# Own buffers for the opening's loads, output decay on the outputs and a reordered slot in a retention plus softplus-FFN kernel

## The chip, the core and the metric

The kernel runs on one core of a Trainium2 chip. The metric is the device time of one execution in microseconds (us). Three timed runs of the kernel before gave 914.02 to 916.24 us, median 914.99 us. A hardware profile of one further execution is read below; that execution took 915.2 us.

The engines, with the names the profile uses: PE (TensorE matmul; PEld is its weight load), DVE (VectorE), ACT (ScalarE), POOL (GpSimd) and SP (SyncE, which here issues every DMA). Each engine executes its own instruction list strictly in order, so an instruction that waits holds everything behind it on that engine.

## The reference

```python
scores = (q @ k.T) / sqrt(64)                    # 8 batches, 8 heads, 576 positions, head size 64
ret    = scores * gamma[h] ** (i - j)  (0 where j > i)
attn   = ret @ v
x      = attn.transpose(0, 2, 1, 3).reshape(4608, 512)
h      = x @ w_in                                # 512 -> 2048
g      = max(h, 0) + log1p(exp(-abs(h)))         # softplus
out    = g @ w_out                               # 2048 -> 512
```

All in float32. The decay gamma^(i-j) factors into gamma^(i+1), which belongs to the query position, and gamma^-(j+1), which belongs to the key/value position.

## The kernel before

**Attention** is done in *steps*: 36 chunks of 128 tokens times two halves of the heads give 72 steps. A step m loads one block `raw` of 128x1152 floats (keys, queries, keys by position, values; 576 KB). On PE it needs `scores` (lines 150 and 155: eight 64x64 score products and up to eight state sums k'v, all into one PSUM tile) and `values` (lines 204 and 214: scores times v, then queries times the carried state). DVE turns the score tile into the masked `a` (L168) and the sums into `u`, `sx` and the carried state `s` (L181 to L193); POOL copies half of the old state into `sx` (L177) and decays `s` (L195). `values_out` writes the result as a rounded head (ACT, L229) and the remainder (DVE, L233) into `xt`, the input of the FFN. `scale_next` multiplies the queries (L127) and, from step 9 on, the values (L130) by their decay factors on POOL, in place in `raw`; for steps 0 to 8 ACT scales the values (L140).

**The FFN** runs in 144 *slots*, 16 for each unit of 512 tokens. Slot i does 12 matmuls `h` (L248), then Abs, Exp, Ln on ACT (L256 to L258), the softplus sum on DVE (L262), a rounded head `g` on ACT (L266) and its remainder on DVE (L267). After the `h` matmuls of slot i, PE does the 12 `y` matmuls (L280) of slot i-1. In every odd slot one attention step is put ahead of `h`: scores of step m, values of step m-1.

**The weights** come as 32 pieces of 512 KB in a raw form. Each piece passes `weight_a` (ACT Prelu L309, DVE L311), `weight_b` (DVE L317), `weight_c` (ACT head L325) and `weight_d` (DVE remainder L330). In the text below these are p (L309), t (L311), b, c and d. Three raw buffers `wst` take turns; the load of piece n+3 is issued behind d of piece n. Pieces 0 to 2 begin in the opening; slot i handles pieces 3+2i and 4+2i, so slots 0 to 14 carry weight work.

**The stages.** The *opening* is steps 0 to 8 before slot 0. The *weight slots* are slots 0 to 14. The *plain slots* follow. The order of the work is written out by hand: the program order of each engine is the order of the source. Opening blocks take turns in three `rawp` buffers and two `g` buffers, so a load waits until the block that lay there is used.

Of the kernel before, what the change touches and what calls it, by code (L numbers as in the profile page):

```python
# [19 lines left out]
P = 128  # L20
# [15 lines left out]
SMALL = 2 * QC  # L36
NCONST = NPAIR * QC + H + NPAIR
PIECE = 512
START_WEIGHTS = 3
OPENING = 5  # L40
WBUFS = 3
# [17 lines left out]
def retention_softplus_ffn(ctx: ExitStack, tc, first, others, consts, w, out):  # L59
    nc = tc.nc  # L60

    const = ctx.enter_context(tc.tile_pool(name="const", bufs=1))
    wpool = ctx.enter_context(tc.tile_pool(name="wpool", bufs=1))
    xpool = ctx.enter_context(tc.tile_pool(name="xpool", bufs=2))
    att = ctx.enter_context(tc.tile_pool(name="att", bufs=2))
    moe = ctx.enter_context(tc.tile_pool(name="moe", bufs=2))
# [3 lines left out]
    ps_h = ctx.enter_context(tc.tile_pool(name="ps_h", bufs=2, space=PSUM))  # L70
    ps_att = ctx.enter_context(tc.tile_pool(name="ps_att", bufs=1, space=PSUM))
    rawp = ctx.enter_context(tc.tile_pool(name="rawp", bufs=3))
    weight_pools = ExitStack()
    wst = weight_pools.enter_context(tc.tile_pool(name="wst", bufs=WBUFS))
    later = {}

    consts_sb = const.tile([P, NCONST], F32, name="consts_sb")
    mask = const.tile([P, HC], F32, name="mask")

    decq = [consts_sb[:, n:n + SMALL].rearrange("p (s c) -> p s c", s=2) for n in (0, NCONST - SMALL)]  # L80
    vsc, gchp = consts_sb[:, SMALL:SMALL + H], consts_sb[:, SMALL + H:SMALL + H + NPAIR]


    ws = [wpool.tile([P, 2, 2 * PIECE], F32R, name=f"w{p}") for p in range(NF)]
# [17 lines left out]
    def load_step(m):  # L102

        pool, tag = (moe, "g") if m in (3, 4, 8) else (rawp, "rawp")
        r = pool.tile([P, RAW], F32, tag=tag, name=f"raw_{tag}")
        if m == 0:
            for to, at in ((consts_sb, slice(0, SMALL + H + NPAIR)), (r, slice(0, KQ)), (r, slice(KQ, RAW)),
                           (consts_sb, slice(NCONST - SMALL, NCONST))):
                nc.sync.dma_start(to[:, at], (first if to is r else consts)[:, at])
        else:  # L110
            nc.sync.dma_start(r, others[m - 1])
        kq, kv = r[:, 0:KQ], r[:, KQ:]
        k = kq[:, 0:2 * C].rearrange("p (s c) -> p s c", s=2)
        q = kq[:, 2 * C:].rearrange("p (s c) -> p s c", s=2)
        kv = kv.rearrange("p (a s c) -> p a s c", a=2, s=2)
        live[m] = dict(k=k, q=q, kp=kv[:, 0], v=kv[:, 1])

    scaled = [0]

    def scale_next():  # L120

        m = scaled[0]
        if m not in live:
            return
        scaled[0] += 1
        q = live[m]["q"]
        nc.gpsimd.tensor_mul(q, q, decq[m % 2])  # L127
        if m >= AHEAD:
            v, f = value_scale(m)
            nc.gpsimd.tensor_mul(v, v, f.unsqueeze(2).broadcast_to([P, 4, D]))  # L130

    def value_scale(m):
        return live[m]["v"].rearrange("p s (h d) -> p (s h) d", h=2), vsc[:, 4 * (m % 2):4 * (m % 2) + 4]

    def scale_values(m):

        if m < AHEAD:
            v, f = value_scale(m)
            for n in range(4):
                nc.scalar.activation(v[:, n], v[:, n], AF.Copy, scale=f[:, n:n + 1])  # L140

    def scores(m, bank):

# [4 lines left out]
        for s in range(2):  # L148
            for t, h in quads:
                nc.tensor.matmul(bank[rows[t], h, SCOLS][:, part[s]], L["k"][rows[h], s, part[t]],  # L150
                                 L["q"][rows[h], s, part[t]], start=True, stop=True, skip_group_check=True)
        for s in range(2):
            for t, h in quads:
# [353 lines left out]
```

## Time and profile before

| what | value |
|---|---|
| median of three timed runs | 914.99 us |
| the profiled execution: own time / span of the trace | 915.2 us / 913.5 us |
| busy share: PE / PEld / DVE / ACT / POOL | 98% / 80% / 41% / 48% / 18% |
| h matmuls: count, busy | 1740, 426.1 us |
| y matmuls: count, busy | 1728, 415.9 us |
| HBM read / written | 59.64 MB / 9.44 MB |

The shares are averages over stages with different limits: PE is short of work only in the first 130 us. The stage table and the chain of waits in the rows below show that.

### The profile page before, as it was taken

To read this page: it belongs to the slowest core of one execution; us is meant where nothing else is said; L and a number is where in the kernel's file an instruction comes from. 1 tells how busy PE (TensorE), PEld (TensorE's weight loads), DVE (VectorE), ACT (ScalarE), POOL (GpSimd) and SP (SyncE) were. 2 spreads that over 40 slices of the span, in tenths; PEclk is the share of its full clock that TensorE was granted. 3 is DMA by queue.
4 is the path that set the end of the run, shared out by engine and by line. 5 is a ranking of instruction groups with operands and counts; after the bars stand their busy time and mean duration, and the time that the engine had idled before them with its cause. 6 is when DMAs were issued, how large, how long until landed. Compare 5 with 4: busy or idle time off the path is not lost.

```text
span 913.5 us, 18133 instructions
## 1 busy us (share of the span) xinstructions
PE 892.7 (98%) x7830; PEld 726.4 (80%) x7830; DVE 376.1 (41%) x745; ACT 440.9 (48%) x775; POOL 164.8 (18%) x270
## 2 busy tenths in 40 slices
PE   7699999999999999999999999999999999999998
PEld 6577778888888888888888888888888888888886
DVE  5689984333333343333433343334333333332222
ACT  5577774444444444444444444444444444445444
POOL 5322221111111111111221111111211121100000
PEclk7799999999999999999999999999999999999999
DMA  8556642111211112111211121112111121001001
GB/s 289 204 187 213 206 153 98 36 45 52 99 52 53 53 66 65 48 53 52 99 53 52 52 80 48 52 54 99 52 53 53 39 88 53 27 1 47 1 1 46
DMA packets 20671, 70.24 MB, mean 77 GB/s; under 512 B 2288, under 2 KB 2544, under 8 KB 20592
## 3 DMA queue, kind: packets, MB, share of 16 engines
q1 hardware_dynamic: 20592, 69.09, 22.9%
q8 instruction: 61, 1.00, 0.5%
q14 instruction: 18, 0.15, 0.1%
HBM read 59.64 MB, written 9.44 MB: 76 GB/s over the span
## 4 chain that ended last, share of the span: by engine, by line
PE 88%; DVE 5%; DMA 3%; ACT 3%; POOL 1%; issue 0%; SPq 0%; POOLq 0%; DVEq 0%; ACTq 0%
PE h L248 41%; PE y L280 40%; PE bank L150 2%; DMA raw_rawp<-others 2%; PE bank L214 2%; PE bank L204 2%; PE bank L155 1%; DMA wst<-w 1%; DVE g L267 1%; DVE wst L317 1%; DVE w L330 1%; DVE wst L311 1%; ACT w L325 1%; POOL raw_rawp L127 1%; DVE ab L262 0%; ACT ab L257 0%
## 5 line engine op out<-in xcount | busy, mean ns | idle before, releaser
L248 PE MATMUL h<-xt,w 128*128 128x512 f32 (+1 forms) x1740 | 426.1, 394 | 0.9 <-DVE w L330 0.8
L280 PE MATMUL y<-w,g 128*128 128x512 f32 x1728 | 415.9, 390 | 3.1 <-DVE g L267 3.1
L280 PEld LDWEIGHTS y<-w,g 128*128 128x128 f32 x1728 | 323.7, 188 | 73.2 <-DVE g L267 5.3
L248 PEld LDWEIGHTS h<-xt,w 128*128 128x128 f32 x1740 | 320.3, 188 | 71.7 <-DVE w L330 3.3
L262 DVE SCALAR_TENSOR_TENSOR ab<-h,ab 128x512 f32<-128x512 f32 (+1 forms) x145 | 99.7, 688 | 408.2 <-ACT ab L258 408.1
L256 ACT ACTIVATE ab<-h 128x512 f32<-128x512 f32 (+1 forms) x145 | 86.3, 595 | 295.1 <-PE h L248 295.1
L267 DVE TENSOR_TENSOR g<-ab,g 128x512 fp32r<-128x512 f32 (+1 forms) x145 | 104.2, 718 | 90.7 <-ACT g L266 89.2
L266 ACT CAST g<-ab 128x512 fp32r<-128x512 f32 (+1 forms) x145 | 89.5, 617 | 100.1 <-DVE ab L262 98.8
L127 POOL TENSOR_TENSOR raw_rawp<-raw_rawp,consts_sb 128x384 f32<-128x384 f32 x69 | 72.3, 1048 | 193.1 <-DMA raw_rawp<-others 186.7
L195 POOL TENSOR_TENSOR s<-s,consts_sb 128x128 f32<-128x128 f32 x64 | 25.7, 401 | 419.7 <-DVE s L193 372.4
L258 ACT ACTIVATE ab<-ab 128x512 f32<-128x512 f32 (+1 forms) x145 | 91.2, 629 | 4.6
L257 ACT ACTIVATE ab<-ab 128x512 f32<-128x512 f32 (+1 forms) x145 | 91.2, 629 | 4.6
L130 POOL TENSOR_TENSOR raw_rawp<-raw_rawp,consts_sb 128x256 f32<-128x256 f32 x63 | 41.5, 659 | 0.0
L229 ACT CAST xt<-bank 128x256 fp32r<-128x256 f32 x68 | 25.3, 372 | 30.4 <-PE bank L214 30.3
L150 PEld LDWEIGHTS bank<-raw_rawp 64*64 64x64 f32 x1008 | 20.4, 133 | 22.2 <-issue 22.2
L214 PE MATMUL bank<-raw_rawp,sx 64*64 64x64 f32 x472 | 27.8, 221 | 4.3 <-POOL sx L177 4.3
L204 PE MATMUL bank<-a,raw_rawp 64*64 64x64 f32 x1056 | 30.6, 223 | 0.0
L168 DVE TENSOR_TENSOR a<-bank,mask 128x256 f32<-128x256 f32 x63 | 26.6, 423 | 9.6 <-ACT xt L229 9.5
L233 DVE TENSOR_TENSOR xt<-bank,xt 128x256 fp32r<-128x256 f32 x68 | 28.3, 416 | 3.8 <-ACT xt L229 3.7
L150 PE MATMUL bank<-raw_rawp 64*64 64x64 f32 x1008 | 29.1, 230 | 0.0
L309 ACT ACTIVATE wst<-wst 128x512 f32<-128x512 f32 x32 | 21.8, 682 | 13.3 <-DMA wst<-w 13.3
L155 PE MATMUL bank<-raw_rawp 64*64 64x64 f32 x888 | 25.9, 218 | 0.0
(74 smaller groups left out, 422.4 us busy)
## 6 DMA issues: line engine op xcount, KB each, us to landing
raw_rawp<-others SPq DMA_DIRECT2D x68, 576.0 KB, 4.1
wst<-w SPq DMA_DIRECT2D x32, 512.0 KB, 3.9
out<-osb SPq DMA_DIRECT2D x36, 256.0 KB, 2.4
raw_g<-others SPq DMA_DIRECT2D x3, 576.0 KB, 7.8
raw_rawp<-first SPq DMA_DIRECT2D x1, 320.0 KB, 3.1
raw_rawp<-first SPq DMA_DIRECT2D x1, 256.0 KB, 4.4
consts_sb<-consts SPq DMA_DIRECT2D x1, 198.0 KB, 2.3
consts_sb<-consts SPq DMA_DIRECT2D x1, 192.0 KB, 4.6
```

The lines of the kernel that those rows point to most:

```text
L127: nc.gpsimd.tensor_mul(q, q, decq[m % 2])
L150: nc.tensor.matmul(bank[rows[t], h, SCOLS][:, part[s]], L["k"][rows[h], s, part[t]], L["q"][rows[h], s, part[t]], start=True, stop=True, s ...
L204: nc.tensor.matmul(o[t][rows[h], part[s]], L["v"][rows[t], s, rows[h]], L["a"][rows[t], h, s], start=(s == 0), stop=L["states"][t] is None ...
L214: nc.tensor.matmul(o[t][rows[h], part[s]], lhs[rows[t], s], rhs, start=False, stop=True, skip_group_check=True)
L248: nc.tensor.matmul(h, ws[p][:, a, kt * P:(kt + 1) * P], xt[:, b, kt, cols], start=(n == 0), stop=(n == 3 * NKT - 1))
L256: nc.scalar.activation(ab, h, AF.Abs)
L257: nc.scalar.activation(ab, ab, AF.Exp, scale=-1.0)
L258: nc.scalar.activation(ab, ab, AF.Ln, bias=1.0)
L262: nc.vector.scalar_tensor_tensor(ab, h, 0.0, ab, op0=ALU.max, op1=ALU.add)
L266: nc.scalar.copy(g[:, HI], ab)
L267: nc.vector.tensor_sub(g[:, LO], ab, g[:, HI].bitcast(F32))
L280: nc.tensor.matmul(y, g[:, a, at:at + P], ws[p][:, b, PIECE:], start=(p == 0 and n == 0), stop=(p == NF - 1 and n == 2))
```

## The change

1. **Loads of the opening.** Steps 0 to 10 get buffers of their own (`openp`, `NOPEN` = 11), at the place in SBUF where weight tiles 8 to 15 are put later, once step 11 is reached. Step 0 and the constants it needs come as two DMAs, `part0` and `part1`. From step 11 on two `rawp` buffers (before: three) take turns, and the load of step m+1 is issued in the slot of step m.
2. **Decay on the outputs.** The POOL multiplication of the queries (L127 before, 128x384, 72 of them) is gone. `values_out` now multiplies the PSUM result by the decay on DVE into a tile `x` (128x256); ACT rounds the head from `x`, and the remainder is subtracted on POOL (on DVE for step 7 alone).
3. **Four raw weight buffers** (before: three); pieces 0 to 3 are loaded in the opening.
4. **Order of a slot.** In the weight slots t of piece n+1 is moved up next to b of piece n, the step's DVE work stands behind the softplus sum instead of ahead of the slot, and d of piece n-1 stands between the logarithm and the softplus sum. In the plain slots the step's DVE work stands behind `h` in the program.
5. PE does the same instructions in the same order, with three idle matmuls at the start instead of five.

```diff
-OPENING = 5
-WBUFS = 3
+OPENING = 3
+NOPEN = AHEAD + 2
+WBUFS = 4
 def load_step(m):
-        pool, tag = (moe, "g") if m in (3, 4, 8) else (rawp, "rawp")
-        r = pool.tile([P, RAW], F32, tag=tag, name=f"raw_{tag}")
...
+            if m < NOPEN:
+                r = openp.tile([P, RAW], F32, name=f"raw{m}")
+            else:
+                r = rawp.tile([P, RAW], F32, tag="rawp", name="rawp")
...
-    def scale_next():
...
-        q = live[m]["q"]
-        nc.gpsimd.tensor_mul(q, q, decq[m % 2])
...
+    def values_out(m, bank, rest):
...
+        x = att.tile([P, 2, C], F32, tag="x", name="x")
+        nc.vector.tensor_mul(x.rearrange("p s (t c) -> p s t c", t=2),
+                             bank[:, :, VCOLS].rearrange("p t (s c) -> p s t c", s=2),
+                             constant[0][2][:, pr:pr + 2].rearrange("p s (t c) -> p s t c", t=2))
+
+        def parts_out():
+            nc.scalar.copy(hi, x)
+            rest.tensor_sub(lo, x, hi.bitcast(F32))
+        return parts_out
...
     for i in range(NSLOT):
+        weight_p(n)
+        weight_t(n)
+        weight_c(n - 1)
+        weight_b(n)
+        weight_t(n + 1)
         h = hidden_mm(i)
         ab = logs(h)
+        weight_dl(n - 1)
         softplus(h, ab)
-        weight_cd(n)
+        if step and n < NPIECE:
+            parts_out = values_out(m - 1, bank, nc.gpsimd)
+            scores_out(m)
+            states_out(m)
+            if NOPEN <= m + 1 < NSTEP:
+                load_step(m + 1)
+            scale_values(m + 1)
+        weight_c(n)
+        weight_dl(n)
         gs[i] = [softplus_split(ab)]
-        weight_a(n + 1)
+        softplus_rest(gs[i][0], ab)
+        if step and n < NPIECE:
+            parts_out()
+        weight_p(n + 1)
         weight_b(n + 1)
```

The order of the instructions at two places. First POOL at the end of the opening, before. The names ending in a number are buffers: `raw_rawp_478` is the block of step 9, `sx_545` the state half that values of step 7 read.

```order
L127 TENSOR_TENSOR raw_g_364<-raw_g_364,consts_sb_85 128x384
L177 COPY sx_487<-s_380 64x128
L195 TENSOR_TENSOR s_492<-s_492,consts_sb_85 128x128
L127 TENSOR_TENSOR raw_rawp_478<-raw_rawp_478,consts_sb_85 128x384
L130 TENSOR_TENSOR raw_rawp_478<-raw_rawp_478,consts_sb_85 128x256
L177 COPY sx_545<-s_434 64x128
```

The same place of the changed program, on POOL; `raw_543` is the block of step 9.

```order
L247 TENSOR_TENSOR xt_216<-x,xt_216 128x2x128
L194 COPY sx<-s 64x128
L212 TENSOR_TENSOR s<-s,part_91 128x128
L247 TENSOR_TENSOR xt_216<-x,xt_216 128x2x128
L194 COPY sx<-s 64x128
L212 TENSOR_TENSOR s<-s,part_91 128x128
L145 TENSOR_TENSOR raw_543<-raw_543,part_91 128x256
```

The block of step 9 stood ahead of the `sx` copy of step 7 and now stands behind every `sx` and `s` of the opening; a remainder (L247) has come into each step.

Second DVE in an odd weight slot, before, from the step's first operation to the remainder `g`. `ab` is the softplus sum, `w_91` a finished weight tile.

```order
L168 TENSOR_TENSOR a<-bank,mask 128x256
L184 TENSOR_TENSOR u<-bank,s 128x128
L185 TENSOR_TENSOR sx<-bank,s 64x128
L193 TENSOR_TENSOR s<-bank,u 128x128
L233 TENSOR_TENSOR xt_669<-bank,xt_669 128x2x128
L311 TENSOR_SCALAR wst<-wst 128x512
L330 TENSOR_TENSOR w_93<-wst,w_93 128x512
L317 SCALAR_TENSOR_TENSOR wst<-wst 128x512
```

The changed program, DVE, an odd weight slot from its d of the earlier piece on.

```order
L355 TENSOR_TENSOR w_99<-wst,w_99 128x512
L276 SCALAR_TENSOR_TENSOR ab<-h,ab 128x512
L241 TENSOR_TENSOR x<-bank,consts_sb 128x256
L178 TENSOR_TENSOR a<-bank,mask 128x256
L201 TENSOR_TENSOR u<-bank,s 128x128
L202 TENSOR_TENSOR sx<-bank,s 64x128
L210 TENSOR_TENSOR s<-bank,u 128x128
L355 TENSOR_TENSOR w_99<-wst,w_99 128x512
L284 TENSOR_TENSOR g<-ab,g 128x512
```

Before, the five operations of the step stand ahead of the slot's weight work and its softplus sum; now they stand between the softplus sum and the remainder `g`, with one d.

## Rows read from the trace of the kernel before

**Rows 1.** Windows by stage: start:end, length, busy of each engine, PE clock, DMA share, GB/s

```profile
0.00:33.71 33.71, 20.72 (x531) 18.12 (x531) 17.91 (x52) 16.88 (x55) 18.26 (x33) 0.68 0.83 284
33.71:38.66 4.95, 4.95 (x63) 3.82 (x61) 3.19 (x7) 1.74 (x4) 2.76 (x5) 0.76 0.21 51
38.66:131.81 93.15, 89.12 (x772) 68.58 (x768) 82.44 (x145) 70.37 (x121) 22.27 (x28) 1.00 0.59 195
131.81:814.10 682.29, 682.29 (x6047) 556.53 (x6041) 245.29 (x501) 306.55 (x521) 121.47 (x205) 1.00 0.18 59
```

**Rows 2.** Chain that ended last, end of the opening: start, length, what

```profile
23.45 6.64 DMA raw_rawp<-others
...
31.88 0.30 POOL sx L177
...
33.78 4.04 PE h L248 x12
```

**Rows 3.** Windows, two us of the opening with five loads queued

```profile
10.00:12.00 2.00, 2.00 (x82) 2.00 (x82) 1.02 (x4) 1.53 (x7) 1.91 (x3) 0.50 1.05 429
```

**Rows 4.** Timeline of the opening, ACT, then DVE: start, length, line, operation

```profile
9.97 1.06 ACT L140 ACTIVATE raw_rawp<-raw_rawp,consts_sb 128x64 f32<-128x64 f32 x4 [0.34 <-DMA raw_rawp<-others]
...
20.49 0.41 DVE L168 TENSOR_TENSOR a<-pair,mask 128x256 f32<-128x256 f32 x1
...
21.65 1.05 DVE L330 TENSOR_TENSOR w<-wst,w 128x512 fp32r<-128x512 f32 x1
...
23.02 0.41 DVE L168 TENSOR_TENSOR a<-pair,mask 128x256 f32<-128x256 f32 x1
```

**Rows 5.** Windows, a pair of weight slots, then a pair of plain slots

```profile
65.96:80.27 14.31, 12.89 (x118) 9.79 (x112) 12.38 (x23) 10.75 (x19) 3.07 (x4) 1.00 0.58 192
...
144.11:156.30 12.19, 12.19 (x113) 9.95 (x113) 5.20 (x11) 5.75 (x11) 1.59 (x2) 1.00 0.39 136
```

**Rows 6.** Waits from 34 to 132 us: engine, line, releaser, total, times, longest

```profile
DVE ab L262 <- ACT ab L258: 5.7, 7, 2.6
...
ACT wst L309 <- DMA wst<-w: 13.3, 13, 2.6
```

**Rows 7.** Groups by line, 38.66 to 131.81 us: busy, mean ns, idle before

```profile
L267 DVE TENSOR_TENSOR g<-ab,g 128x512 fp32r<-128x512 f32 x14 | 13.2, 946 | 0.7
...
L127 POOL TENSOR_TENSOR raw_rawp<-raw_rawp,consts_sb 128x384 f32<-128x384 f32 x7 | 8.9, 1278 | 15.2 <-DMA raw_rawp<-others 13.0 <-ACT w L325 2.2
L130 POOL TENSOR_TENSOR raw_rawp<-raw_rawp,consts_sb 128x256 f32<-128x256 f32 x7 | 7.1, 1020 | 0.0
```

**Rows 8.** Timeline around slot 9, DVE, ACT, POOL

```profile
94.28 0.69 DVE L267 TENSOR_TENSOR g<-ab,g 128x512 fp32r<-128x512 f32 x1
...
96.03 0.42 DVE L168 TENSOR_TENSOR a<-bank,mask 128x256 f32<-128x256 f32 x1
...
96.72 0.59 ACT L256 ACTIVATE ab<-h 128x512 f32<-128x512 f32 x1
...
97.53 0.59 DVE L311 TENSOR_SCALAR wst<-wst 128x512 int32<-128x512 uint32 x1
98.03 0.68 DVE L330 TENSOR_TENSOR w<-wst,w 128x512 fp32r<-128x512 f32 x1
98.64 0.68 DVE L317 SCALAR_TENSOR_TENSOR wst<-wst 128x512 int32<-128x512 int32 x1
...
100.13 1.47 POOL L127 TENSOR_TENSOR raw_rawp<-raw_rawp,consts_sb 128x384 f32<-128x384 f32 x1 [2.30 <-DMA raw_rawp<-others]
...
100.65 1.50 DVE L267 TENSOR_TENSOR g<-ab,g 128x512 fp32r<-128x512 f32 x1
```

**Rows 9.** Chain that ended last, plain slots

```profile
144.11 2.95 PE h L248 x12
147.06 2.72 PE y L280 x12
```

**Rows 10.** DMA issues from 40 to 130 us: count, KB, median us to landing

```profile
wst<-w SPq DMA_DIRECT2D x26, 512.0 KB, 3.8
```

More of the change, by code (lines that the diff above doesn't have):

```diff
@@ L116, in load_step, with scale_values, sums @@
         live[m] = dict(k=k, q=q, kp=kv[:, 0], v=kv[:, 1])
-    scaled = [0]
-    def scale_next():
-        m = scaled[0]
-        if m not in live:
+    def scale_values(m):
+        if m >= NSTEP:
             return
-        scaled[0] += 1
-        q = live[m]["q"]
-        nc.gpsimd.tensor_mul(q, q, decq[m % 2])
+        v = live[m]["v"].rearrange("p s (h d) -> p (s h) d", h=2)
+        f = constant[0][0][:, 4 * (m % 2):4 * (m % 2) + 4]
         if m >= AHEAD:
-            v, f = value_scale(m)
             nc.gpsimd.tensor_mul(v, v, f.unsqueeze(2).broadcast_to([P, 4, D]))
[L132 to L140, printed above, removed]
-    def scores(m, bank):
+            return
+        for n in range(4):
+            nc.scalar.activation(v[:, n], v[:, n], AF.Copy, scale=f[:, n:n + 1])
+    def scores(m, bank):
+        if m >= NSTEP:
+            return
+        L = live[m]
+        for s in range(2):
+            for t, h in quads:
+                nc.tensor.matmul(bank[rows[t], h, SCOLS][:, part[s]], L["k"][rows[h], s, part[t]],
+                                 L["q"][rows[h], s, part[t]], start=True, stop=True, skip_group_check=True)
+        L["bank"] = bank
+    def sums(m):
         if m >= NSTEP:
@@ L149, in scores @@
             for t, h in quads:
[L150 to L153, printed above, removed]
                 if follows if t else start != HC:
-                    nc.tensor.matmul(bank[rows[h], t, TCOLS][:, part[s]], L["kp"][rows[t], s, rows[h]],
+                    nc.tensor.matmul(L["bank"][rows[h], t, TCOLS][:, part[s]], L["kp"][rows[t], s, rows[h]],
                                      L["v"][rows[t], s, rows[h]], start=True, stop=True, skip_group_check=True)
-        L["bank"] = bank
     def scores_out(m):
@@ L347, in retention_softplus_ffn @@
                                 fill=0.0, base=0, channel_multiplier=-1)
[L349 to L359 removed]
+    idle = ps_val.tile([P, 2, T], F32, tag="val", name="idle")
     for n in range(OPENING):
[L361 removed]
@@ L362, in retention_softplus_ffn @@
-    scale_next()
-    scale_next()
+        nc.tensor.matmul(idle[:, 0, 0:2 * C], fill[:, 0:P], fill[:, 0:2 * C], start=True, stop=True)
     scale_values(0)
     for m in range(AHEAD):
-        pair = ps_open.tile([P, 2, 4 * C], F32, tag="pair", name="pair")
-        if m % 2:
-            both, vbanks = None, [ps_h.tile([P, 4 * C], F32, tag="h", name="hv") for _ in range(2)]
-        elif m:
-            both = ps_att.tile([P, 2, 4 * C], F32, tag="bank", name="bank")
-            vbanks = [both[:, n] for n in range(2)]
-        rest = lambda: None
+        pair = ps_open.tile([P, 2, T], F32, tag="pair", name="pair")
@@ L385, in retention_softplus_ffn @@
[L385 removed]
+            sums(m)
+            values_out(m - 1, bank, nc.vector)()
+        if m < AHEAD - 1:
+            scale_values(m + 1)
         scores_out(m)
+        states_out(m)
         if 0 < m < AHEAD - 1:
[L388 to L401 removed]
@@ L405, in retention_softplus_ffn @@
     weight_b(2)
-    open_pools.close()
+    scale_values(AHEAD)
+    psum_pools.close()
+    ps_h = ctx.enter_context(tc.tile_pool(name="ps_h", bufs=2, space=PSUM))
     ps_y = ctx.enter_context(tc.tile_pool(name="ps_y", bufs=1, space=PSUM, side="right"))
+    constant[0] = constants(consts_sb[:, 0:SMALL], consts_sb[:, SMALL:])
     for i in range(NSLOT):
+        n = START_WEIGHTS + 2 * i
         m = AHEAD + (i - 1) // 2
-        if i % 2 and m <= NSTEP:
-            both = ps_att.tile([P, 2, 4 * C], F32, tag="bank", name="bank")
-            scores(m, both)
-            values(m - 1, [both[:, n] for n in range(2)])
-            rest = values_out(m - 1, both)
-            scores_out(m)
-            rest()
-            load_next()
-            scale_next()
+        step = i % 2 and m <= NSTEP
+        if step:
+            bank = ps_att.tile([P, 2, T], F32, tag="bank", name="bank")
+            scores(m, bank)
+            sums(m)
+            values(m - 1, bank)
+        weight_p(n)
+        weight_t(n)
+        weight_c(n - 1)
+        weight_b(n)
+        weight_t(n + 1)
```

202 lines of the change are left out of this document (100 added, 102 removed).

## The prediction

> **What bounds the kernel now.** I read the windows by stage first, then the chain of waits, then the waits and the timeline of the two stages in which PE is short of work. In the plain slots PE is busy 682.29 of 682.29 us [rows 1]: nothing but fewer or faster matmuls helps there, and the change leaves PE's list as it is, except for two idle matmuls at the very start. A pair of plain slots takes 12.19 us [rows 5]. PE's missing time lies earlier. The opening lasts 33.7 us with PE busy 20.72 at a granted clock of 0.68, and the next stage, seven pairs of weight slots from 38.66 to 131.81 us, takes 93.15 us [rows 1]. That is 13.31 us for a pair, 1.12 more than the plain pair, 7.8 us in all. So two things can be won: an earlier slot 0, and up to 7.8 us in the weight slots. All sums are made against the profiled execution, which took 915.2 us (span 913.5); the median of the runs is 0.2 lower, less than their spread.
>
> What ends the opening is a wait, not work. The chain goes through a load of a raw block issued at 23.45 that takes 6.64 us, then to an `sx` copy on POOL at 31.88, then to the first `h` at 33.78 [rows 2]. The order says why: POOL scales queries and values of step 9 ahead of the `sx` copy that values of step 7 read, so slot 0 waits for the block of step 9, which it does not use. That block in turn was issued late, because it had to wait for a buffer.
>
> In the weight slots DVE is nearly the bound: 82.44 us in seven pairs, 11.78 a pair [rows 1], so it is idle 1.53 us of a pair's 13.31. In the worst pair PE is busy 12.89 of 14.31 us [rows 5].
>
> **The opening, step by step.** Every block now has a buffer, so SP issues them back to back. When five loads stood in the queue, the DMA moved 429 GB/s [rows 3], against a mean of 284 over the opening [rows 1]. Up to the block of step 2 the new queue holds 1990 KB (326 + 512 + 2 x 576), the old one 2118 KB, and there it landed by 9.97 us [rows 4]; I take 9.7. From there to the block of step 8 are five more steps' blocks, one more for step 8 and three weight pieces, 6 x 576 + 3 x 512 = 4992 KB or 5.11 MB. At 429 GB/s that is 11.9 us, so the last block lands at 21.6; at 284 GB/s 18.0 us, so 27.7.
>
> By then DVE is the slower. A step with one weight operation took 2.53 us there, from 20.49 to 23.02, with the weight operation at 1.05 us [rows 4], which elsewhere takes 0.68 [rows 8]. The new step has the same number of DVE operations: the remainder goes to POOL, the decay product comes. No row shows that product; from below it is a 128x256 product out of PSUM like the mask, 0.42 us [rows 8], the same as the remainder it replaces, and since its second operand comes from SBUF as the mask's does I take that value. From above it could run at the rate of a disturbed operation, 1.05/0.68 of that, or 0.65; then six steps cost 1.4 us more. So a step costs 2.53 us as disturbed as before, or 2.16 with the weight operation undisturbed. Step 2 begins on DVE about 11.5 (9.7, plus ACT's 1.06 for the values [rows 4], plus its sums on PE). Steps 2 to 7 end at 11.5 + 6 x 2.16 = 24.5, or at 11.5 + 6 x 2.53 = 26.7. Then come the decay product (0.42) and ACT's head (I take 0.4, the length of the DVE operations of that size): `h` of slot 0 starts between 25.3 and 27.5. I take 26.4. Against 33.78 that is 7.4 us. The two ends outside this: if the queue gives only 284 GB/s, the last block lands at 27.7, ACT scales its values (1.06) before it rounds the heads of steps 6 and 7 (2 x 0.4), and `h` starts at 29.5, a gain of 4.3.
>
> The first `h` group took 4.04 us at the lower clock, against 2.95 later [rows 2, 9]; the granted clock of its stretch was 0.76, between the levels of 1.2 and 2.4 GHz, after a PE that had waited some microseconds. The new opening keeps PE busier just before, so the clock may already be up; that would be another 1.1 us. I count nothing for it, and it belongs to the lower end.
>
> The removed query product (1.0 us each on POOL undisturbed) was the first thing on the way to the scores of each step. In the opening it is no more waited for; in the plain slots it lay beside PE, so its absence brings nothing there. Two idle matmuls less, and constants packed with the first block: nothing, since PE waits for the first block either way.
>
> **The weight slots.** DVE's own work stays: the decay product for the remainder, as above. What changes is first the disturbance by POOL. A remainder `g` takes 0.69 us alone, and 1.50 while POOL works through the query product, which itself takes 1.47 [rows 8]; the mean of 14 is 946 ns [rows 7]. POOL gives up 8.9 us of query products and gains a 128x256 subtraction, which no row shows; the value product of that size took 7.1 us in all [rows 7]. So POOL's 22.27 us [rows 1] become about 20.5, 8% less, and DVE's 11.78 perhaps 11.7 a pair.
>
> The Trainium skill, SBUF — State Buffer, section "Who interferes with whom", says that VectorE with two SBUF inputs and a GpSimd instruction that reads SBUF hold a shared port by exclusive lock: who starts first has it for its whole instruction, and the other blocks. The overlap at 100.13 agrees that they disturb each other, but there both became longer. The rule speaks against the change in one point, which is a rival below: the new subtraction is on POOL and reads two SBUF tiles.
>
> Second, DVE's waits. It waits 5.7 us in seven pairs for the logarithm [rows 6], 0.81 a pair, and ACT waits 13.3 us for raw weights to land [rows 6], which holds b, c and d behind it. The fourth buffer gives each load a whole piece's time more (3 us, a quarter of a pair) against a median landing of 3.8 us [rows 10], so these waits should go; t and d moved into DVE's wait for the logarithm fill part of it. I leave 0.9 us of the 1.53 idle. A pair becomes 11.7 + 0.9 = 12.6 us, seven pairs save 7 x 0.71 = 5.0. Bounds: PE's own 12.19 (7.8 saved) and no change (0 saved).
>
> What is late next is the odd slot's chain. From the start of one `y` that waited to the next: `y` 2.72 and the following `h` 2.95 [rows 9], the attention matmuls between them (1.1, the 12.19 of a pair less two `h` and two `y` groups), ACT's three functions (96.72 to the end of the third at 98.6, so 1.95), the softplus sum (0.60), the five step operations that now stand here (96.03 to 97.53, 1.50), d (0.61, 98.03 to 98.64) and the remainder (0.62, the 0.69 less its overlap) [rows 8]: together 12.05. It is just under 12.19, so it binds only when POOL disturbs it.
>
> **The plain slots.** Loads look one step ahead rather than further: issue behind the values of step m-1, landing and POOL's value product must be done before the next sums 11 us later (12.19 less the attention's 1.1). With 6.64 us for landing, the long one of the chain [rows 2], and 1.0 for the product [rows 7] that still leaves 3 us. Nothing changes there, nor at the end.
>
> **Sum.** 915.2 - 7.4 - 5.0 = 902.8 us.
>
> **The rivals.**
> A. The queue does not hold its rate: 284 GB/s, slot 0 at 29.5. For it: the mean of the opening; against it: that mean contains the times when SP waited for buffers. 915.2 - 4.3 - 5.0 = 905.9 us.
> B. The weight slots gain nothing, because the chain above is disturbed: if POOL's subtraction or value product meets d or `g` there, it adds 0.81 (1.50 - 0.69) or twice that, so 12.9 to 13.7, about today's 13.31. For it: the chain has only 0.14 us to spare. Against: POOL scales the next block's values first, and that block lands only about 5 us after its issue, behind `g`. 915.2 - 7.4 = 907.8 us. By the lock of the Trainium skill, SBUF — State Buffer, section "Who interferes with whom", each meeting would cost DVE up to POOL's whole operation, 1.02 us by the mean of the value product [rows 7], and so give much the same time.
> C. The weight slots gain all and the first `h` runs at the full clock: 915.2 - 7.4 - 7.8 - 1.1 = 898.9 us. For it: PE, not DVE, has the larger sum (12.19 against 11.7). Against: DVE in a list this full has waits.
> D. Slower: t is moved a whole slot ahead of its d and now blocks DVE itself until its piece has landed (before, only ACT waited). From t to d of one piece DVE has two d, the softplus sum, the five step operations, `g`, two b and two t to do, some 6 us by the lengths above, so a buffer has the other 6.2 us of a pair for its load. If a landing took longer, all of DVE would stop, and the softplus sum behind it. To lose the opening's 7.4 us, a pair must take over 14.4 us (13.31 + 7.4/7), which needs landings above 8.4 us. At 9 us: 915.2 - 7.4 + 7 x (12.2 + 2.8 - 13.31) = 919.6 us. For it: the DMA share is 0.59 in this stage and ACT did wait 2.6 us once; against it: the median of 3.8 us.
>
> **How the numbers follow.** The forecast's case 0.52, A 0.15, B 0.18, C 0.10, D 0.03, and 0.02 for nothing visible, a gain in one stage given back in the other. A difference of 0.2%, 1.8 us, is about what a measurement of this kernel can tell from no change. All of A, B, C and the forecast lie beyond it: faster 0.95, same 0.02, slower 0.03. The range goes from C's time to somewhat over B's, 898.5 to 909.0; the rest, about 0.13, lies mostly with A and B together (915.2 - 4.3 = 910.9) and with D.
>
> **What would show it.** In the changed trace the first `h` should start near 26.4 us, DVE should be over 90% busy from 12 us to there, and no `sx` wait should stand in the chain. Windows over pairs of weight slots should show 12.6 us, DVE 11.7, and ACT's wait for raw weights near nothing. Plain pairs should stay at 12.19. The forecast is wrong if the first `h` is later than 28, if weight pairs stay above 13.1, or if any plain pair is longer.

## The result and the profile after

| | before | after |
|---|---|---|
| median of the runs taken together (lowest to highest) | 915.62 us (914.02 to 917.46) | 906.29 us (905.15 to 907.14) |
| ratio of the two, 95% interval | | 0.9897 [0.9873, 0.9921] |
| profiled execution: own time / span | 915.2 / 913.5 us | 907.14 / 905.4 us |

(The runs of before are the three shown ahead and one more beside the changed kernel.) The change makes the kernel about 9.3 us faster; 12.4 were forecast. The time lies within the range. The two profiled spans differ by 8.1 us, and all that follows accounts for those.

First the windows by stage, cut where the stages of before were cut (the first `h` itself starts 0.06 us ahead of the first cut): start:end, length, busy time of PE, PEld, DVE, ACT and POOL with their instructions, granted clock, DMA share, GB/s.

```profile
0.00:25.99 25.99, 17.01 (x527) 14.20 (x527) 15.89 (x46) 15.46 (x48) 10.59 (x28) 0.93 0.81 318
25.99:34.38 8.39, 6.35 (x61) 4.58 (x61) 6.17 (x14) 5.66 (x10) 2.91 (x5) 0.70 0.83 287
34.38:123.79 89.41, 88.12 (x771) 69.95 (x769) 78.06 (x144) 68.53 (x118) 21.18 (x27) 0.99 0.58 189
123.79:806.00 682.21, 682.21 (x6042) 556.86 (x6041) 239.00 (x500) 308.20 (x519) 109.47 (x209) 1.00 0.18 60
```

Set beside [rows 1]: the opening is 7.72 us shorter (33.71 to 25.99), the way from slot 0 to slot 1 is 3.44 us *longer* (4.95 to 8.39), the seven weight pairs are 3.74 us shorter (93.15 to 89.41), and the plain slots are unchanged (682.29 to 682.21). 7.72 - 3.44 + 3.74 + 0.08 = 8.10. In the second row PE is busy 6.35 of 8.39 us: here is a wait that the forecast has no term for.

The chain of waits from slot 0 to slot 1 (start, length, what):

```profile
25.42 0.11 DVE w L355
...
26.58 5.94 DMA raw<-others
...
32.66 0.69 PE bank L156 x16
```

Where [rows 2] had a 6.64 us load and POOL's `sx` ahead of slot 0, the chain now has a 5.94 us load ahead of slot 1. It is block 9, whose scores stand in front of `h` of slot 1. It is issued only at 26.58. SP's list says why (timeline of SP: start, time from the first instruction of the row to the end of the last, line, operation, count):

```profile
11.44 15.09 SPq L319 DMA_DIRECT2D wst<-w  x3
26.58 0.72 SPq L131 DMA_DIRECT2D raw<-others  x1
```

The third of these weight loads is that of piece 5, which the source puts behind d of piece 1, and d of piece 1 is the L355 row at 25.42 above. The load of block 9 has its own buffer and could have gone at any time, but stands behind that wait on the same queue. The timeline of PE and PEld shows the price:

```profile
25.93 4.70 PE L262 MATMUL h<-xt,w 128*128 128x512 f32 x12
27.00 3.19 PEld L262 LDWEIGHTS h<-xt,w 128*128 128x128 f32 x10 [0.57 <-ACT xt L246]
...
32.66 0.69 PE L156 MATMUL bank<-raw 64*64 64x64 f32 x16 [2.04 <-DMA raw<-others]
34.38 3.83 PE L262 MATMUL h<-xt,w 128*128 128x512 f32 x12
```

PE waits 2.04 us, and behind the wait its clock is at the lower of the two levels of 1.2 and 2.4 GHz: the granted clock is 0.52 from 32.66 to 36.20 us, and the second group of `h` takes 3.83 us against 2.95 in [rows 9]. The first group stands ahead of that wait, and its length has other grounds: its third matmul waits 0.57 us for ACT's head of step 7, and the granted clock is 0.50 from 25.90 to 29.30 us. Its 4.70 us are 0.66 more than in [rows 2], so of the 3.44 us some 2.8 are the price of block 9.

Now the weight slots. The waits from 26 to 124 us (engine, line, releaser: total, times, longest):

```profile
DVE ab L276 <- ACT ab L272: 8.9, 9, 2.8
...
PE bank L156 <- DMA raw<-others: 2.0, 1, 2.0
DVE wst L336 <- DMA wst<-w: 1.5, 3, 0.8
PE y L296 <- DVE g L284: 1.3, 6, 0.2
```

ACT's 13.3 us for raw weights [rows 6] are gone; what is left of them is 1.5 us on DVE, where t of the later piece now stands ahead of its p. PE waits for `g` in six of the seven pairs, 0.2 us each. The wait itself is the smaller part: `y` that waited takes 2.94 us instead of 2.72 from its start to the next group's (106.95 to 109.89). Its first weight load starts together with its first matmul, where that of a `y` that did not wait starts 0.22 us ahead (100.92 against 101.14). So PE counts as busy 12.5 us in such a pair and has still only 12.2 us of work (windows of two pairs of weight slots):

```profile
72.88:85.58 12.70, 12.49 (x118) 9.88 (x112) 11.43 (x23) 9.97 (x17) 3.03 (x4) 1.00 0.61 212
98.28:110.98 12.70, 12.49 (x119) 9.88 (x112) 11.63 (x22) 9.93 (x17) 3.25 (x4) 1.00 0.61 214
```

What `y` waits for is one chain, without a gap (chain of waits in the second of these pairs, then two rows of PE's timeline):

```profile
101.34 0.61 ACT ab L270
...
103.34 0.57 issue
103.91 0.41 DVE x L241
104.32 0.33 DVE a L178
...
105.20 0.29 DVE s L210
105.49 0.60 DVE w L355
106.09 0.81 DVE g L284
```

```profile
106.95 3.01 PE L296 MATMUL y<-w,g 128*128 128x512 f32 x12 [0.21 <-DVE g L284]
110.98 3.02 PE L262 MATMUL h<-xt,w 128*128 128x512 f32 x12
```

From `y` to the next `h` it is 4.03 us (106.95 to 110.98), from there to ACT's first function 3.06 (98.28 to 101.34), ACT's three functions 1.96, the softplus sum 0.61 (the "issue" row is most of it), the five step operations 1.58, d 0.60, `g` 0.80, and 0.06 to the next `y`: 12.70, the length of the pair. DVE has 78.06/7 = 11.15 us of work in a pair and is not the bound.

Groups by line, 34.38 to 123.79 us (busy, mean ns, idle before), the answer to [rows 7]:

```profile
L284 DVE TENSOR_TENSOR g<-ab,g 128x512 fp32r<-128x512 f32 x14 | 11.1, 794 | 0.6
L247 POOL TENSOR_TENSOR xt<-x,xt 128x256 fp32r<-128x256 f32 x7 | 7.1, 1008 | 0.0
L241 DVE TENSOR_TENSOR x<-bank,consts_sb 128x256 f32<-128x256 f32 x7 | 2.9, 415 | 0.0
```

`g` has come down from 946 to 794 ns, the decay product is at 415 ns, and POOL's new subtraction at 1008 ns is about as long as its value product.

Last, PE in the opening (timeline) has two gaps that nothing in the profile releases:

```profile
15.00 0.35 PE L156 MATMUL pair<-raw 64*64 64x64 f32 x9 [1.52 <-issue]
20.90 0.39 PE L156 MATMUL pair<-raw 64*64 64x64 f32 x10 [2.95 <-issue]
```

They lie 127 matmuls apart, each with its own weight load; with the two semaphore instructions of PE that the trace has between them these are 256 instructions. The trace also has a DMA queue of the kind "instruction": 61 packets with 1.00 MB, 16.4 KB each. PE has 2 x 7826 matmuls and weight loads, and 15652/256 = 61.1. Each packet stands in the trace with its time: one runs from 12.58 to 13.52 us, the next from 18.57 to 19.54, and PE goes on 1.48 and 1.36 us after their ends. So I read these gaps as PE waiting for the next piece of its own instruction list. The Trainium skill, Runtime: NRT & Kernel Launch, section "Instruction fetch mechanics", says that an engine's sequencer fetches its instructions by a DMA queue of its own in blocks of 256, the cost mostly hidden; distance and packets agree with the blocks, the 1.52 and 2.95 us show that here it was not hidden.

### The profile page after: what moved, and what is told of

It is laid out like the page before. It is cut to its first block, busy times and chain, and to the rows that moved or that the text cites. A ratio compares the mean times of both kernels' runs of the same rounds, so it can differ in the third digit from the quotient of the medians.

```text
span 905.4 us, 18152 instructions
## 1 busy us (share of the span) xinstructions
PE 889.3 (98%) x7826; PEld 724.9 (80%) x7826; DVE 366.4 (40%) x742; ACT 443.3 (49%) x771; POOL 144.9 (16%) x269
## 4 chain that ended last, share of the span: by engine, by line
PE 92%; DVE 4%; DMA 2%; ACT 1%; issue 1%; SPq 0%; DVEq 0%
PE h L262 43%; PE y L296 41%; PE bank L156 3%; PE bank L220 2%; PE bank L231 2%; PE bank L169 2%; DMA raw<-others 1%; DVE w L355 1%; DVE g L284 1%; DMA wst<-w 0%; DVE x L241 0%; DVE a L178 0%; ACT ab L272 0%; ACT ab L271 0%; ACT ab L270 0%
## 5 line engine op out<-in xcount | busy, mean ns | idle before, releaser
L262 PE MATMUL h<-xt,w 128*128 128x512 f32 (+1 forms) x1740 | 426.7, 395 | 0.0
L262 PEld LDWEIGHTS h<-xt,w 128*128 128x128 f32 x1740 | 321.8, 189 | 69.1 <-ACT xt L246 0.6
L284 DVE TENSOR_TENSOR g<-ab,g 128x512 fp32r<-128x512 f32 (+1 forms) x145 | 101.3, 699 | 90.6 <-ACT g L280 89.2
L247 POOL TENSOR_TENSOR xt<-x,xt 128x256 fp32r<-128x256 f32 x71 | 54.6, 769 | 470.8 <-ACT xt L246 470.5
L246 ACT CAST xt<-x 128x256 fp32r<-128x256 f32 x72 | 29.2, 406 | 68.3 <-DVE x L241 68.3
L145 POOL TENSOR_TENSOR rawp<-rawp,consts_sb 128x256 f32<-128x256 f32 x61 | 39.9, 655 | 110.2 <-DMA rawp<-others 110.2
L156 PEld LDWEIGHTS bank<-rawp 64*64 64x64 f32 x976 | 19.8, 133 | 21.5 <-issue 21.5
L212 POOL TENSOR_TENSOR s<-s,consts_sb 128x128 f32<-128x128 f32 x55 | 23.9, 435 | 60.5 <-DVE s L210 49.3
L156 PE MATMUL bank<-rawp 64*64 64x64 f32 x976 | 28.2, 231 | 0.0
L350 ACT CAST w<-wst 128x512 fp32r<-128x512 f32 x32 | 21.2, 663 | 13.5 <-DVE wst L342 13.3
L220 PE MATMUL bank<-a,rawp 64*64 64x64 f32 x976 | 27.3, 220 | 0.0
L241 DVE TENSOR_TENSOR x<-bank,consts_sb 128x256 f32<-128x256 f32 x64 | 26.7, 418 | 0.0
L231 PE MATMUL bank<-rawp,sx 64*64 64x64 f32 x440 | 25.2, 218 | 0.0
L169 PE MATMUL bank<-rawp 64*64 64x64 f32 x864 | 25.2, 218 | 0.0
```

The costliest lines, as they stand in the source:

```text
L169: nc.tensor.matmul(L["bank"][rows[h], t, TCOLS][:, part[s]], L["kp"][rows[t], s, rows[h]], L["v"][rows[t], s, rows[h]], start=True, stop=T ...
L220: nc.tensor.matmul(bank[rows[h], t, VCOLS][:, part[s]], L["v"][rows[t], s, rows[h]], L["a"][rows[t], h, s], start=(s == 0), stop=L["states ...
L247: rest.tensor_sub(lo, x, hi.bitcast(F32))
L262: nc.tensor.matmul(h, ws[p][:, a, kt * P:(kt + 1) * P], xt[:, b, kt, cols], start=(n == 0), stop=(n == 3 * NKT - 1))
L284: nc.vector.tensor_sub(g[:, LO], ab, g[:, HI].bitcast(F32))
```

## The experiments

Three questions: does the load of block 9 cost the 3.4 us; what holds the weight pairs at 12.7 us; and what are the gaps without a releaser. Each ratio is to the kernel before in the same job (its medians: 916.22, 915.70 and 915.85 us), with a 95% interval. Edits are against the changed kernel, unless said otherwise.

### Block 9 loaded ahead of the weight loads that wait

```diff
+    load_step(AHEAD)
+    nc.sync.dma_start(consts_sb, consts)
+    load_step(AHEAD + 1)
     nc.gpsimd.memset(mask, 1.0)
-        if m == AHEAD - 2:
-            load_step(AHEAD)
-            nc.sync.dma_start(consts_sb, consts)
-            load_step(AHEAD + 1)
```

> The loads of steps 9 and 10 and of the constants are issued in the opening behind weight piece 3, instead of behind the loads of pieces 4 and 5, which wait for a weight buffer. Theory (slot 1 of the changed kernel waits for the block of step 9, because its load stands on SP behind a load that waits for d of piece 1): PE's 2.0 us wait goes, the sums' wait for the scaled values with it, and h of slot 1 no longer runs at the lower clock (3.83 against 3.02 us): about 3 us less than the changed kernel, 903. Rival (something else, the values of step 8 or the weight piece 2, is ready no earlier): within 1 us of the changed kernel, 906.

906.82 us, 0.9899 [0.9886, 0.9913]: no gain. PE's timeline:

```profile
26.94 0.38 PE L220 MATMUL bank<-a,raw 64*64 64x64 f32 x9 [2.17 <-issue]
28.20 4.38 PE L262 MATMUL h<-xt,w 128*128 128x512 f32 x12
33.43 3.04 PE L262 MATMUL h<-xt,w 128*128 128x512 f32 x12
```

The wait for block 9 is gone, and slot 0 to slot 1 takes 5.23 us (28.20 to 33.43) instead of 8.45 (25.93 to 34.38). So the theory holds for the place. But a third gap without a releaser, 0.28 us of PEld in the changed kernel, is now 2.17 us, and slot 0 is later by 2.3. Slot 1 comes only 0.95 us earlier. The seven pairs behind, where `y` waits eight times instead of six, take 89.73 us instead of 89.41, so some 0.6 us are left in the profile and nothing that shows in the medians. The size was wrong: the stretch is 3.2 us shorter in its place, and next to nothing is won in the kernel.

### POOL's order alone, in the kernel before

```diff
         scale_values(m + 1)
-        scale_next()
+        if scaled[0] < AHEAD:
+            scale_next()
...
     weight_b(2)
+    scale_next()
+    scale_next()
```

> The kernel before, with POOL's scaling of steps 9 and 10 moved behind the opening's last state decay, and nothing else. Theory (half of the opening's gain is POOL's order, not the buffers): values of step 7 run at about 28 us, h of slot 0 starts near 29.5 instead of 33.8, slot 1 still needs the block of step 9 that lands at 30 and its scaling of 1.6 us, so some 3.5 to 4.5 us less than before, 911. Rival (without own buffers the opening stays where it was, the buffers carry it all): under 1 us, 915.

912.78 us, 0.9961 [0.9947, 0.9975]. The first `h` starts at 30.33 instead of 33.71:

```profile
30.33 4.99 PE L248 MATMUL h<-xt,w 128*128 128x512 f32 x12
36.16 3.02 PE L248 MATMUL h<-xt,w 128*128 128x512 f32 x12
```

So the reading of [rows 2] was right: the block of step 9, scaled ahead of `sx`, held slot 0. This order alone is 3.4 of the 7.7 us of the opening. The rest lies with the other parts of the change, the product that left POOL (next experiment) and the buffers of the blocks; the buffers alone were not tried.

### The query product put back

```diff
+    ones = const.tile([P, HC], F32, name="ones")
+    nc.gpsimd.memset(ones, 1.0)
...
+        nc.gpsimd.tensor_mul(q, q, ones.unsqueeze(1).broadcast_to([P, 6, HC]))
         v = live[m]["v"]
```

> The query multiplication is put back on POOL in place, where it stood before, but by ones (128x384), beside the decay on the outputs; all else as changed. Theory (the decay on the outputs is what took POOL off the way to the scores and off DVE's back): every step of the opening waits another 1.0 us for POOL before its scores, h of slot 0 starts 1.5 to 3 us later, and the weight slots have 1.3 us more of POOL in a pair: 3 to 6 us more than the changed kernel, 909 to 912. Rival (POOL has room and the opening is DVE's): within 1.5 us, 906.

910.78 us, 0.9951 [0.9939, 0.9963], 4.5 us more than the changed kernel. Slot 0 starts at 29.16, 3.2 us later. PE's timeline at slot 1 and seven pairs on, then the waits from 26 to 124 us:

```profile
35.98 3.02 PE L264 MATMUL h<-xt,w 128*128 128x512 f32 x12
...
127.31 3.02 PE L264 MATMUL h<-xt,w 128*128 128x512 f32 x12
```

```profile
PE bank L158 <- POOL raw L143: 1.9, 1, 1.9
...
PE y L298 <- DVE g L286: 1.5, 6, 0.3
...
PE bank L233 <- POOL sx L196: 1.0, 1, 1.0
...
PE h L264 <- DVE w L357: 0.9, 3, 0.4
```

From slot 0 to slot 1 it is 6.82 us instead of 8.45, so at slot 1 only 1.6 of the 3.2 us are left; the seven pairs take 91.33 us instead of 89.41. So taking the product off POOL is worth about half of the change, not quite half of that up to slot 1 and the rest in the pairs; in the forecast it had no term of its own. The product stands here beside a subtraction that POOL did not have before, so this is its price in the changed kernel and not in the one before.

### Three raw weight buffers

```diff
-WBUFS = 4
+WBUFS = 3
```

(and without the early load of piece 3)

> Three raw weight buffers instead of four, and piece 3 loaded behind d of piece 0 as in the kernel before; all else as changed. Theory (the fourth buffer is what the weight slots needed): DVE now waits for landings at t, a pair goes from 12.7 to 13.2 us or more, 3.5 us slower than the changed kernel, 910. Rival (the new order carries the gain): under 1 us, 907.

918.32 us, 1.0025 [1.0016, 1.0035]: slower than before, 12 us above the changed kernel. The waits from 26 to 124 us:

```profile
ACT wst L329 <- DMA wst<-w: 19.8, 12, 2.9
DVE wst L336 <- DMA wst<-w: 17.8, 18, 1.4
...
PE h L262 <- DVE w L355: 5.8, 6, 1.3
...
PE y L296 <- DVE g L284: 2.7, 5, 0.8
```

Pairs take 13.8 to 15.3 us. t stands far ahead of its d now, so with three buffers DVE itself waits for landings (17.8 us). This is rival D's mechanism, and its place; the fourth buffer is what kept it from happening. How much the fourth buffer alone would bring to the kernel before wasn't tried.

### The step behind `g`

```diff
-        if step and n < NPIECE:
-            parts_out = values_out(m - 1, bank, nc.gpsimd)
-            scores_out(m)
...
         softplus_rest(gs[i][0], ab)
+        if step and n < NPIECE:
+            parts_out = values_out(m - 1, bank, nc.gpsimd)
+            scores_out(m)
...
```

> In the odd weight slots the five step operations on DVE stand behind the remainder g instead of between the softplus sum and d. Theory (the chain y, attention, h, logarithm, sum, step, d, g sets the pair of weight slots at 12.7 us): the chain becomes some 1.6 us shorter, PE's 12.2 us bound takes over, a pair takes 12.2 to 12.4 us and the whole 2.3 to 3.7 us less than the changed kernel, 903. Rival (DVE's total with its disturbed operations, or the landing of the weights, sets 12.7): the pair stays at 12.6 to 12.8 and the time within 1 us, 906.

911.14 us, 0.995 [0.9936, 0.9963]. `y` waits for `g` no more, but the load of the next block moved with the step and now comes too late: PE waits 2.6 us for blocks and 1.4 for POOL's value product, and three pairs take 14.5 to 15.2 us. Two things changed at once, so this run decides nothing. The next leaves the load in front:

```diff
+        if step and n < NPIECE and NOPEN <= m + 1 < NSTEP:
+            load_step(m + 1)
         weight_c(n)
```

> As the run with the step's five DVE operations behind the remainder g, but the load of the next step's block keeps the place it has in the changed kernel. Theory (that run lost its time to blocks that were loaded too late, PE waited 2.6 us for their DMA and 1.4 for POOL's product, while its waits for g were gone): now neither wait is there, a pair takes 12.2 to 12.5 us, 2 to 3.5 us less than the changed kernel, 903.5. Rival (DVE's total sets the pair at 12.7): within 1 us of the changed kernel, 906.

904.65 us, 0.9875 [0.9861, 0.9889]. `y` does not wait, some pairs take 12.2 to 12.3 us, the seven 88.68. In others `h` waits for d instead (`PE h L262 <- DVE w L355`, 1.1 us in three), since d of the later piece now stands behind the step, and once PE waits 1.2 us for a block.

### The step ahead of the slot, as before, all else as changed

```diff
             values(m - 1, bank)
+        if step and n < NPIECE:
+            parts_out = values_out(m - 1, bank, nc.gpsimd)
+            scores_out(m)
+            states_out(m)
+            parts_out()
+            if NOPEN <= m + 1 < NSTEP:
+                load_step(m + 1)
+            scale_values(m + 1)
...
         weight_p(n)
```

> In the weight slots the step's DVE work and its load go back to where they stood before, ahead of the slot's weight work; four raw buffers, t moved up and all else as changed. Theory (the chain through the softplus sum, the step and g sets the pair at 12.7 us): the step leaves the chain, the waits of y for g go and a pair takes 12.2 to 12.5 us, 1.5 to 3.5 us less than the changed kernel, 903 to 905. Rival (the place between the sum and g was the right one, since the step ahead of the slot delays b, t and d): a pair takes 12.9 or more, 907 or more.

903.81 us, 0.9874 [0.9859, 0.9888], the lowest of all. No `y` waits. The windows of the seven pairs and of two:

```profile
33.73:121.35 87.62, 87.57 (x770) 70.34 (x768) 79.15 (x146) 68.88 (x120) 21.08 (x27) 0.98 0.60 197
...
47.31:59.52 12.21, 12.21 (x117) 9.96 (x113) 10.97 (x21) 9.42 (x18) 2.83 (x4) 1.00 0.59 196
84.44:96.74 12.30, 12.30 (x118) 9.89 (x113) 11.50 (x21) 9.72 (x19) 3.38 (x4) 1.00 0.66 212
```

87.62 us for the seven pairs against 89.41: the moved place of the step, with the load that goes with it, costs 1.8 us there, and the rest of the change is worth 5.5 (93.15 to 87.62). With the 1.58 us of the step out of the chain, PE's own work sets the pair: it is busy 87.57 of the 87.62 us. That is the theory of the odd chain, shown by taking a piece out of it. Against the changed kernel the ratios overlap, so the version is better by its windows, by 2.5 us in the medians, and not by an interval of its own.

### The remainder back on DVE

```diff
-            parts_out = values_out(m - 1, bank, nc.gpsimd)
+            parts_out = values_out(m - 1, bank, nc.vector)
```

> In the weight slots the remainder of the step's output is subtracted on DVE (behind g) instead of on POOL. Theory (POOL's subtraction disturbs DVE's operations in the chain that sets the pair): g's mean falls from 794 ns to about 700, a pair gets 0.1 to 0.25 us shorter, total 1 to 2 us less, 904.5 to 905.5. Rival (DVE's own work counts, not the disturbance): 0.4 us more on DVE in a pair, total 0 to 3 us more, 906 to 909.

907.53 us, 0.9908 [0.9893, 0.9923]: no difference from the changed kernel that shows. DVE and POOL around the chain's end (timelines):

```profile
104.24 0.71 POOL L212 TENSOR_TENSOR s<-s,consts_sb 128x128 f32<-128x128 f32 x1 [8.83 <-DVE s L210]
...
104.61 0.89 DVE L284 TENSOR_TENSOR g<-ab,g 128x512 fp32r<-128x512 f32 x1
105.42 0.41 DVE L247 TENSOR_TENSOR xt<-x,xt 128x256 fp32r<-128x256 f32 x1
```

`g` is as long as with the subtraction on POOL (mean 785 against 794 ns), `y` waits six times for 1.3 us in all, as before the edit, and a pair stays at 12.70. So rival B's cause is excluded: the subtraction runs behind `g` and touches nothing on the chain. Nor does the value product, B's other candidate: in the changed kernel's pair it starts at 108.08 us, where `g` has ended at 106.89. What lies beside `g` here is POOL's decay of the state, L212; whether it is what lengthens `g` wasn't tried.

### The gaps without a releaser

64 more matmul records ahead of the opening:

```diff
+    for n in range(32):
+        nc.tensor.matmul(idle[:, 0, 0:32], fill[:, 0:P], fill[:, 0:32], start=True, stop=True)
```

> 32 more idle matmuls of 32 columns at the start of PE's list, before the first block has landed; all else as changed. They are 64 records, half of the 128 matmul records that lie between the two places in the opening where PE stood still for 1.5 and 2.95 us with no wait that the profile shows. Theory (PE stands there until the next piece of its instruction list is read, behind the queued loads): the two stalls move 64 matmul records earlier in the program, to other operations, and stay 1 to 3 us each; the total stays within 1.5 us. Rival (these two places wait for data): the stalls stay at the sixth to eighth score matmul of steps 4 and 6.

914.20 us, 0.998 [0.9971, 0.9988]; the idle matmuls took 13.70 us, far more than I gave them, and delay everything by some 9 us. The places still answer (timeline of PE):

```profile
23.63 0.34 PE L156 MATMUL pair<-raw 64*64 64x64 f32 x8 [1.46 <-issue]
27.28 0.38 PE L156 MATMUL pair<-raw 64*64 64x64 f32 x9 [0.93 <-issue]
```

These are the scores of steps 3 and 5, where the changed kernel has its gaps at steps 4 and 6. A step is 64 matmul records, so the gaps moved in the program by what was put ahead of it, and the instruction queue has 62 packets instead of 61. Counted with the weight loads and the few semaphore instructions, 449 instructions of PE stand ahead of the first gap in both kernels, and 705 ahead of the second. A gap fixed to a count of instructions, not to a tile or a time, is the reading of the list. The packets end at 22.12 and 25.94 us, and PE goes on 1.51 and 1.34 us later. The DMA had drained here (12 GB/s from 21 to 24 us), and the second gap is shorter, 0.93 against 2.95 us.

Two loads held back until a buffer is free, then four:

```diff
-                r = openp.tile([P, RAW], F32, name=f"raw{m}")
+                at = m - 6 if m in (7, 8) else m
+                r = openp.tile([P, RAW], F32, tag=f"raw{at}", name=f"raw{at}")
```

> The blocks of steps 7 and 8 take the buffers of steps 1 and 2, so that their loads and the weight pieces behind them are issued only when values of steps 1 and 2 are done, at about 13 and 15 us instead of 7 and 10. Theory (a queue that is always full delays PE's instruction reads): the DMA is idle now and then from 17 us on, the second stall of 2.95 us shrinks to under 1, h of slot 0 starts 1.5 to 2.5 us earlier than 25.9, total about 904 to 905. Rival (the stall doesn't come from the queue, or these loads land too late now): the stall stays or a wait for these blocks takes its place, total 906 to 909.

905.67 us, 0.9887 [0.9873, 0.9901]. The gaps are unchanged (1.52 and 2.89 us), but so is the DMA, over 400 GB/s up to 22 us: the edit did not empty the queue, and says nothing.

```diff
+                at = m - 4 if 5 <= m <= 8 else m
```

> The blocks of steps 5 to 8 take the buffers of steps 1 to 4, so four loads and what stands behind them on SP are held; the DMA should be idle between about 11 and 13 us and again later. Theory (PE's two stalls are reads of its instruction list, lengthened by a full queue): the stall of 2.95 us becomes 1.5 or less, as in the run with more idle matmuls, where the queue was drained; the loads now come late instead, so the total is 905 to 910. Rival (the queue has no part in it): both stalls keep 1.5 and 2.9 us.

908.03 us, 0.9919 [0.9905, 0.9932]. Now the queue is short at 12 to 14 us (92 and 194 GB/s), and the two gaps are gone; the third one, with the queue full again, has grown:

```profile
27.45 0.38 PE L221 MATMUL bank<-a,raw 64*64 64x64 f32 x9 [2.70 <-issue]
29.06 4.04 PE L263 MATMUL h<-xt,w 128*128 128x512 f32 x12
```

Waits for data (0.7 us for ACT's values, 1.4 for `x`) take the place of the gaps that went, so PE also came later to those places; the run as a whole is no gain. The third place is the cleanest comparison: the same instruction waits 0.28 us (PEld) in the changed kernel, where the DMA moved 8 GB/s from 24 to 27 us and the packet had ended at 23.45, and 2.17, 2.70 and 2.21 us in the three kernels that keep the queue full to about then (block 9 early, four loads held, and the next one). In these three the packet ends at 25.52, 26.01 and 25.10 us, and PE goes on 1.4 to 1.5 us later.

### Block 9 early and the step behind `g`, together

```diff
+    load_step(AHEAD)
+    nc.sync.dma_start(consts_sb, consts)
+    load_step(AHEAD + 1)
...
         softplus_rest(gs[i][0], ab)
+        if step and n < NPIECE:
+            parts_out = values_out(m - 1, bank, nc.gpsimd)
...
```

> Both edits that looked useful together: blocks 9 and 10 and the constants loaded in the opening, and the step's DVE work behind g with the load of the next block at its place. Theory (the two remove different waits): PE's 1.6 us for the block of step 9 and the waits for g are both gone, 902 to 904. Rival (the full queue stretches PE's instruction reads in the opening and eats the first): 904 to 905.

907.48 us, 0.9912 [0.9898, 0.9926]: the two do not add. The third gap is 2.21 us, slot 0 starts at 27.81, and `h` waits for d four times, 1.6 us in all.

## Why the prediction was right or wrong

**The opening: the time right, in part by luck.** `h` of slot 0 starts at 25.93; 26.4 was forecast, 25.3 to 27.5 allowed. The forecast had it behind the decay product and head of step 7; two of its matmuls do not need them, and the third, which does, starts at 27.00. The queue held its rate (417 GB/s from 8 to 16 us), so rival A is out. Two terms were off and nearly cancelled. Step 2 begins on DVE at 10.51 instead of 11.5, and the six steps from there to the decay product at 26.10 took 2.60 us each, more than the 2.16 to 2.53:

```profile
10.51 0.42 DVE L178 TENSOR_TENSOR a<-pair,mask 128x256 f32<-128x256 f32 x1
...
26.10 0.41 DVE L241 TENSOR_TENSOR x<-bank,part 128x256 f32<-128x256 f32 x1
```

DVE was not over 90% busy either, as the prediction's sign had it: 9.33 of 12 us between 12 and 24, since PE stood still for 4.5 us in the two gaps that no row of before had shown. So DVE's work did not set these steps alone.

**From slot 0 to slot 1: the step that failed.** "Every block now has a buffer, so SP issues them back to back" was taken as true for all eleven. It is not for blocks 9 and 10: they stand on SP behind a weight load that waits for d of piece 1. The prediction ended its sum of the opening at the first `h`, let the next stretch stand at 4.95 us, and so missed 3.44 us, some 2.8 of them block 9's. Of the 4.3 us by which the profiled span was forecast too short (12.4 - 8.1) this is by far the largest part. The order of SP's list was there to be read, and the prediction itself asks who is queued behind a wait, for DVE, ACT and POOL. Without that wait (the first experiment) the stretch is 5.23 us. That this brings no gain that shows is a second effect, the third gap.

**The weight slots: the waits went as forecast, but another bound set the pair.** 12.6 us were forecast for a pair, 5.0 us in all; it was 12.77 in the mean and 3.74 us. The forecast let DVE set it, with 11.7 of work and 0.9 idle, and put the odd chain at 12.05, just under PE's 12.19. DVE has 11.15 and is idle 1.6, the chain has 12.70 and sets the pair; that the two sizes lie so near is luck. Its terms against the forecast: `y` and attention 4.03 for 3.82, `h` 3.06 for 2.95, the five operations 1.58 for 1.50, `g` 0.80 for 0.62, and 0.06 of handing over, together 0.64 of the 0.65. (The attention's 1.1 in it does not come out of the subtraction that the forecast names, 12.19 less two `h` and two `y` groups of [rows 9], which gives 0.85; the trace has 1.09, from 109.89 to 110.98, so the value was right.) The `y` of [rows 9] had not waited; one that had is longer by 0.22 us, its uncovered weight load. A chain that is 0.14 us under the bound, with eight terms, should have been counted as the bound. With the step ahead of the slot the pairs behind the first take 12.2 to 12.6 us, so the forecast's 12.6 was to be had.

**Rival B: half right.** The odd chain binds, as it says, but it was not POOL's subtraction that did it, neither by the 0.81 of the rows nor by a lock as the Trainium skill has it (SBUF — State Buffer, "Who interferes with whom"): without that subtraction on POOL the pair is the same 12.70.

**The small terms.** The decay product: 0.42 forecast, 0.415 measured. ACT's waits for raw weights: near nothing, as forecast, and the three-buffer kernel shows that the fourth buffer does it. The first `h` at full clock was not counted, rightly: it ran at a granted 0.50 for its first 3.4 us. Plain pairs 12.2 and the tail: unchanged, as forecast.

**Rival D** did not come, since the landings stayed at a median of 3.8 us; with one buffer less it does, and then the kernel is slower than before.

## What to carry to other kernels

A load with a buffer of its own is early only if nothing on its queue waits in front of it: go through the queue's list to the first instruction that waits, and price every load behind it, past the stage that the change is about. When a chain of many small terms comes out within a few per cent of the bound, count it as the bound, and take the length of a matmul group from a row where it had waited. And before moving work into a wait, ask whether it lies on the chain that ends there: the step was put behind the softplus sum, ahead of `g`, and delayed `g`, which PE was waiting for.

## What the runs showed of the hardware that was not expected

PE can stop for its own instruction list. The gaps come every 256 instructions, move with the count of instructions, and end 1.3 to 1.5 us after a packet of the instruction queue. At one and the same place they last 0.28 us with the DMA at 8 GB/s and 2.17 to 2.70 us in kernels that keep it loaded to about then. So a faster stream of loads can take back on PE what it gives. In the kernel before PE waited longer for data (5.1 and 3.7 us for `sx` alone), and no such gap is seen. The gap at the first place is 1.06 us with the remainder on DVE and 1.91 with block 9 early, since PE comes there at 13.45 and at 12.62 us; it goes on at 14.51 and 14.53. What sets the start of a packet stays open. In the changed kernel it comes 3.4 and 3.6 us after PE has passed the place 256 instructions ahead of the gap, with the DMA at 420 GB/s, and 1.6 us at the third place, as the queue runs dry; but with four loads held it is 1.5 us at the first place, at 417 GB/s.

Narrow float32 matmuls are not cheap: 64 records with 32 columns and their weight loads took 13.70 us at a granted clock of 1.00, 0.214 us each, hardly less than the 0.227 us (2.72/12) of one with 512 columns in `y` [rows 9]. A weight load of these took 333 ns, one of `y`, whose operands are float32r, 188 ns. Whether that is the reason wasn't tried.
